# Twelve mask products, four k sums and six selection steps per pair of heads, regrouped into fewer, wider VectorE instructions

## The chip, the cores and the metric

One core of a Trainium2 chip runs the whole program. Its engines work side by side, each through its own list of instructions in order: PE (TensorE, matrix products and transposes; PEld is its weight load), DVE (VectorE, element-wise work and reductions), ACT (ScalarE, exponentials, casts and copies), POOL (GpSimd) and SP (SyncE), the last two used here for issuing DMA transfers. The metric is device time in microseconds (us); the kernel before took 453.29, 449.48 and 452.31 in three runs, median 452.31.

## The reference, cut to what matters

Block-sparse attention over batch 4, 8 heads, 768 positions, head size 64, and after it a Fourier mixing layer with a two-layer dense part.

```python
k_rep = k.reshape(B, H, 12, 64, D).mean(axis=3)          # one mean key per block of 64
gate = einsum('bhsd,bhnd->bhsn', q, k_rep)               # 768 x 12 per head
gate = where(pos // 64 >= n, gate, -1e9)
sel = three highest blocks of each row, and its own block
scores = q @ k.T / 8, kept where the block is selected and j <= i, else -1e9
attn = softmax(scores); out = attn @ v
x = out with the heads side by side                      # (4, 768, 512)
u = x + real(fft(fft(x, axis=1), axis=2))
un = layernorm(u)
result = u + relu(un @ w_ch1) @ w_ch2                    # 512 -> 2048 -> 512
```

## The kernel before, in words

Heads are taken two at a time (a pair, `hp`, of heads `e` = 0 and 1), so each of the four batches has four pairs. The 768 positions are six tiles of 128. For one pair:

- `stage_A` transposes q and k on TensorE (six tiles each, three to a PSUM tile), copies q transposed to `qt` (VectorE, fp32) and casts q and k to half precision (ScalarE). VectorE sums each block of 64 keys out of the same PSUM tile into `kr24`, 24 columns: head 0 in rows 0 to 63 and columns 0 to 11, head 1 in rows 64 to 127 and columns 12 to 23, the rest zero (L212, L231 to L235). Four reductions of 64 partitions do it.
- `stage_B` multiplies `qt` with `kr24` to gate scores of both heads, adds the causal term `cz24`, takes the eight largest of each row of 12 (twelve `max`, L251), and for each head turns "at least the third largest, or the own block" into 0 or -60000 in three steps (L252, L255, L256).
- `stage_C` transposes these rows on TensorE and copies them (L266) below the 64 rows of each head's q, so that one product of 76 rows gives scores with the selection in them. The k side holds 0/1 rows there.
- `stage_D_scores` computes the transposed scores, key tile `jt` by query columns, causal part only: 2688 columns a head, laid out by the list `BANKS` in five groups of 512 columns and one of 128, each in one PSUM bank (three buffers). ScalarE takes the exponential of a group in one instruction. Then VectorE multiplies each 128x128 diagonal tile with a triangular 0/1 mask (L293); the six diagonal tiles of a head lie in five of the six groups.
- `stage_D_av` multiplies with v (21 products of 65 columns a head, the last column gives the sums) and divides (L313, L314).

`gen_post` does the mixing of a batch: two products with cosine and sine (L350, L351), the second transform (L371, L372), residual and statistics, a short chain of 6-value instructions for the inverse deviation (L384 to L401), the normalisation (L408), transposes and copies (L415, L417), and the first dense product (L426, L427). `gen_post2` is the second dense product (L441, L443).

`drive` advances these as generators in turn: while batch b's attention runs, batch b-1 is in `gen_post` and batch b-2 in `gen_post2`. Batch 0's attention has only weight loads beside it. After the last attention, `gen_post(3)` runs beside `gen_post2(2)`, and `gen_post2(3)` ends the program. The framework's scheduler puts the instructions of each engine in order when the program is built, by program order and by when it expects operands to be ready, and adds the waits; a PSUM tile is read by ScalarE and VectorE one after the other.

Constants come by DMA. `emit_rest_consts` puts `cz24` and `own01` on the sync queue, behind pair 0's q and k and ahead of pair 2's q and k, which wait for a free buffer (two buffers each).

Of the kernel before, what the change touches and what calls it, by code (L numbers as in the profile page):

```python
# [11 lines left out]
FP = mybir.dt.float32  # L12
F16 = mybir.dt.float16
BF = mybir.dt.bfloat16

NEG = -60000.0
# [3 lines left out]
def _consts_np():  # L20
    S = 768
    DM = 512
    NB = 12
    KH = 386
    s = np.arange(S)
# [16 lines left out]
    own01 = ((s // 64)[:, None] == nn[None, :]).astype(np.float16)  # L42
    IndR = (nn[:, None] == (s[None, :] // 64)).astype(np.float16)
    return dict(CS=CS, SS=SS, CD=CD, SD=SD, ident32=ident32, ident16=ident16,
                ltri=ltri, ut01=ut01, cz24=cz24, own01=own01, IndR=IndR)
# [3 lines left out]
def kernel(  # L49
# [27 lines left out]
    spool = ctx.enter_context(tc.tile_pool(name="small", bufs=8))  # L77
# [12 lines left out]
    own01 = cpool.tile([128, NST, NB], F16, tag="c_own", name="own01")  # L90
# [21 lines left out]
    def emit_rest_consts():  # L112
        nc.sync.dma_start(cz24, dr["cz24"].ap().rearrange("(st p) n -> p st n", p=128))
        nc.sync.dma_start(own01, dr["own01"].ap().rearrange("(st p) n -> p st n", p=128))
# [41 lines left out]
    def emit_attn_dma(b, hp, qk_only=False, v_only=False):  # L156
# [25 lines left out]
        [(0, 0, 512)],  # L182
        [(0, 512, 768), (4, 512, 768)],
        [(1, 128, 640)],
        [(1, 640, 768), (3, 384, 768)],
        [(2, 256, 768)],
        [(5, 640, 768)],
    ]
    OFF = {}
    PT_W = 0  # L190
    for bank in BANKS:
        for (jt, a0, a1) in bank:
            if jt not in OFF:
                OFF[jt] = PT_W - (a0 - 128 * jt)
            PT_W += a1 - a0
    assert PT_W == 2688

    def gen_attention(b):
# [4 lines left out]
        def stage_A(hp):  # L203
# [8 lines left out]
            nc.vector.memset(kr24, 0.0)  # L212
            d["qt"], d["qg"], d["kI"], d["kr24"] = qt, qg, kI, kr24
            for who in range(2):
                src = qn if who == 0 else kn
                for g in range(2):
# [11 lines left out]
                    else:  # L228
                        nc.scalar.copy(out=kI[0][0:64, cols], in_=flat[0:64])
                        nc.scalar.copy(out=kI[1][0:64, cols], in_=flat[64:128])  # L230
                        for e in range(2):  # L231
                            nc.vector.tensor_reduce(
                                out=kr24[64 * e:64 * e + 64, 12 * e + 6 * g:12 * e + 6 * g + 6],
                                in_=ps[64 * e:64 * e + 64].rearrange("p a (x c) -> p a x c", x=2),
                                axis=mybir.AxisListType.X, op=mybir.AluOpType.add)  # L235

        def stage_B(hp):
# [20 lines left out]

        def stage_C(hp):
# [3 lines left out]
            for st in range(NST):  # L263
                nc.tensor.transpose(gt[0:44, st, :], gmp[:, st, :], id16)
# [4 lines left out]
        def stage_D_scores(hp):  # L269
# [5 lines left out]
            for bi, bank in enumerate(BANKS):  # L275
                wid_bank = sum(a1 - a0 for (_, a0, a1) in bank)
                for e in range(2):
# [3 lines left out]
                    diags = []  # L281
                    for (jt, a0, a1) in bank:
# [4 lines left out]
                        if a0 == 128 * jt:  # L287
                            diags.append(po + co)
# [3 lines left out]
                    for dof in diags:  # L292
                        nc.vector.tensor_tensor(out=pt[:, dof:dof + 128], in0=pt[:, dof:dof + 128],  # L293
                                                in1=ut01, op=mybir.AluOpType.mult)
                po += wid_bank

        def stage_D_av(hp):
            d = P[hp]
            v16 = d["v16"]
            for e in range(2):  # L300
# [4 lines left out]
                for jt in range(NST):  # L305
                    for st in range(jt, NST):
                        nc.tensor.matmul(av[:, st, 0:65],  # L307
                                         pt[:, OFF[jt] + 128 * (st - jt):OFF[jt] + 128 * (st - jt) + 128],
# [200 lines left out]
```

## Time and profile before

The profiled execution has a span of 449.5 us from its first to its last instruction; the lowest of the three runs is 449.48, the median 452.31. Mean granted TensorE clock of the core: 0.897 of full speed.

| engine | busy us | share of the span | instructions |
|---|---|---|---|
| PE | 402.2 | 89% | 2806 |
| PEld | 245.3 | 55% | 2806 |
| DVE | 308.3 | 69% | 1059 |
| ACT | 170.0 | 38% | 363 |
| POOL | 41.2 | 9% | 61 |

The chain of work that ended last is 80% PE, 7% DVE, 6% DMA and 5% ACT. Busy time is a sum over stages with different limits; an engine's idle time costs something only where the chain goes through it. PE's ends are modelled, since its instructions are pipelined. Batch 0's attention takes about the first 78 us, batch 1's ends near 159, batch 2's near 259, batch 3's near 358.

### The profile page before, as it was taken

The numbers are of one execution on the slowest core, as the hardware profiler recorded it, in microseconds if no ns is written. First come the engines' busy times: TensorE is split into PE (matmuls) and PEld (weight loads), VectorE is DVE, ScalarE is ACT, GpSimd is POOL, SyncE is SP. The second block draws the span as 40 slices with busy tenths as digits, with TensorE's granted clock in tenths as the row PEclk, the third lists the DMA queues.
The fourth block names the chain that finished last, engine by engine and source line by source line (L and its number), as shares of the span: only waits on it lengthen the run. The fifth ranks groups of instructions, "written<-read, shape, count | busy, mean of one in ns | idle before, by whom it ended". The sixth has DMA issues, their size and how long they took to land.

```text
span 449.5 us, 7427 instructions
## 1 busy us (share of the span) xinstructions
PE 402.2 (89%) x2806; PEld 245.3 (55%) x2806; DVE 308.3 (69%) x1059; ACT 170.0 (38%) x363; POOL 41.2 (9%) x61
## 2 busy tenths in 40 slices
PE   6518999898799999997899999996999999959996
PEld 2517756555466656454566656544665654436542
DVE  0446786799988855688898855688888733477711
ACT  1607678748533343137633244045644110010000
POOL 6705112000011110000001200000000000000000
PEclk9655558999599999999599999998699999969999
DMA  9999994833022262334022264010000011000011
GB/s 164 226 226 185 196 138 26 152 70 69 3 19 19 20 103 73 79 95 94 0 19 20 20 110 115 33 39 4 1 1 2 1 47 48 23 23 1 0 71 71
DMA packets 84980, 29.30 MB, mean 65 GB/s; under 512 B 78064, under 2 KB 80336, under 8 KB 84944
## 3 DMA queue, kind: packets, MB, share of 16 engines
q0 software_dynamic: 29184, 9.73, 18.3%
q1 hardware_dynamic: 52416, 18.28, 17.3%
q10 hardware_dynamic: 3344, 0.82, 1.1%
q8 instruction: 22, 0.36, 0.3%
q14 instruction: 14, 0.11, 0.1%
HBM read 29.87 MB, written 6.29 MB: 80 GB/s over the span
## 4 chain that ended last, share of the span: by engine, by line
PE 80%; DVE 7%; DMA 6%; ACT 5%; issue 1%; SPq 1%; ACTq 0%
DMA qn_2_181<-in_q_dram 3%; DMA id_74<-c_ident 1%; DMA qn_0_99<-in_q_dram 1%; PE ch_5_5338 L441 1%; PE ch_4_5319 L441 1%; PE ch_1_5262 L441 1%; PE ch_4_4879 L441 1%; PE ch_1_4758 L441 1%; PE ch_2_3565 L441 1%; PE ch_1_2230 L441 1%; PE ch_3_5300 L441 1%; PE ch_2_5281 L441 1%; PE ch_5_4918 L441 1%; PE ch_3_4840 L441 1%; PE ch_2_4799 L441 1%
## 5 line engine op out<-in xcount | busy, mean ns | idle before, releaser
L426 PEld LDWEIGHTS <-w_sb 128*128 128x128 f16 x256 | 25.1, 98 | 25.8 <-issue 0.6
L427 PEld LDWEIGHTS <-w_sb 128*128 128x128 f16 x256 | 25.0, 98 | 6.1 <-issue 0.7
L178 POOL DMA_DIRECT2D v_0_0_91<-in_v_dram x4 | 3.4, 854 | 121.0 <-PE av_0_0_2836 L307 65.3
L130 ACT COPY unT_0_4993<-unt_0_5003 128x768 f16<-128x768 f16 x1 | 0.8, 799 | 27.2 <-PE unt_0_5003 L415 27.2
L283 PEld LDWEIGHTS <-kI_1_88 76*128 76x128 f16 x32 | 4.1, 132 | 10.6 <-issue 10.1
L283 PEld LDWEIGHTS <-kI_1_84 76*128 76x128 f16 x32 | 4.1, 131 | 9.7 <-issue 9.2
L220 PE MATMUL tp_2_0_0_302<-id_74,qn_2_181 128*128 128x128 f32 x3 | 0.9, 430 | 9.5 <-DMA qn_2_181<-in_q_dram 9.5
L109 PE MATMUL warmps<-warm_src 128*128 128x512 f16 x22 | 6.9, 486 | 1.2 <-DVE v_0_2_93 L119 1.2
L178 POOL DMA_DIRECT2D v_0_1_92<-in_v_dram x4 | 3.3, 826 | 34.3 <-PE av_1_0_1773 L307 12.3
L283 PEld LDWEIGHTS <-kI_0_87 76*128 76x128 f16 x32 | 3.5, 111 | 4.6 <-issue 2.4
L220 PE MATMUL tp_0_0_0_194<-id_74,qn_0_99 128*128 128x128 f32 x3 | 0.9, 430 | 5.6 <-DMA id_74<-c_ident 5.6
L178 POOL DMA_DIRECT2D v_0_2_93<-in_v_dram x4 | 3.3, 828 | 27.8 <-PE av_2_0_1958 L307 10.8
L415 PE MATMUL unt_0_5003<-id_75,x_3400 128*128 128x128 f16 x6 | 1.7, 288 | 4.5 <-DVE x_3400 L408 4.5
L220 PEld LDWEIGHTS tp_2_0_0_302<-id_74,qn_2_181 128*128 128x128 f32 x3 | 0.5, 213 | 9.6 <-issue 9.6
L283 PEld LDWEIGHTS <-kI_0_83 76*128 76x128 f16 x32 | 3.6, 112 | 3.8 <-issue 1.3
L109 PEld LDWEIGHTS <-warm_src 128*128 128x128 f16 x22 | 2.6, 121 | 5.0 <-issue 2.5
L415 PEld LDWEIGHTS <-x_3400 128*128 128x128 f16 x24 | 2.1, 131 | 5.7 <-DVE x_3400 L408 5.3
L226 ACT CAST qg_0_0_190<-tp_0_0_0_194 64x384 f16<-64x384 f32 x1 | 0.5, 473 | 12.4 <-DVE qT_0_0_189 L225 12.4
L225 DVE COPY qT_0_2_297<-tp_2_0_0_302 128x384 f32<-128x384 f32 x1 | 0.6, 558 | 6.6 <-PE tp_2_0_0_302 L220 6.6
L283 PEld LDWEIGHTS <-kI_2_89 76*128 76x128 f16 x32 | 3.3, 107 | 3.0 <-issue 1.8
L225 DVE COPY qT_0_0_189<-tp_0_0_0_194 128x384 f32<-128x384 f32 x1 | 0.6, 557 | 6.2 <-PE tp_0_0_0_194 L220 6.2
L283 PEld LDWEIGHTS <-kI_2_85 76*128 76x128 f16 x32 | 3.3, 104 | 2.7 <-issue 0.6
(2748 smaller groups left out, 1418.4 us busy)
## 6 DMA issues: line engine op xcount, KB each, us to landing
w_sb<-in_moe_w_ch_dram POOLq DMA_DIRECT2D x8, 256.0 KB, 9.4
w_sb<-in_moe_w_ch_dram POOLq DMA_DIRECT2D x4, 512.0 KB, 16.7
out_dram<-u_943 SPq DMA_DIRECT2D x6, 256.0 KB, 2.4
out_dram<-u_2123 SPq DMA_DIRECT2D x6, 256.0 KB, 2.0
out_dram<-u_3417 SPq DMA_DIRECT2D x6, 256.0 KB, 2.0
out_dram<-u_4694 SPq DMA_DIRECT2D x6, 256.0 KB, 2.0
cs_sb<-c_CS POOLq DMA_DIRECT2D x1, 579.0 KB, 7.5
ss_sb<-c_SS POOLq DMA_DIRECT2D x1, 579.0 KB, 8.8
```

The source lines that it names most:

```text
L109: nc.tensor.matmul(wps, wsrc[:, 0:128], wsrc, start=True, stop=True)
L130: eng.copy(out=dst, in_=src)
L178: nc.gpsimd.dma_start(out=v16_t[e][sl][:, :, 0:64], in_=v[b, h].rearrange("(jt p) d -> p jt d", p=128))
L220: nc.tensor.transpose(ps[:, i, :], src[:, st, :, :].rearrange("p h d -> p (h d)"), id32)
L225: nc.vector.tensor_copy(out=qt[:, cols], in_=flat)
L226: nc.scalar.copy(out=qg[0][0:64, cols], in_=flat[0:64])
L283: nc.tensor.matmul(sp[:, co:co + (a1 - a0)], kI[e][0:76, 128 * jt:128 * (jt + 1)], qg[e][0:76, a0:a1], start=True, stop=True)
L415: nc.tensor.transpose(tps[:, st, :], un16[:, st, 128 * dt:128 * (dt + 1)], id16)
L426: nc.tensor.matmul(ha, w1s, unT[dt][:, 0:512], start=(dt == 0), stop=(dt == NDT - 1))
L427: nc.tensor.matmul(hb, w1s, unT[dt][:, 512:768], start=(dt == 0), stop=(dt == NDT - 1))
L441: nc.tensor.matmul(cps, hT[it][:, 128 * st:128 * (st + 1)], w2_sb[:, it, :], start=(it == 0), stop=(it == NIT - 1))
```

## The change

Three things in the attention part, with the constants that they need.

- The list `BANKS` is rearranged: the first four diagonal tiles of a head fill the first group, the last two stand at the head of the second, and what lies off the diagonal follows. The diagonal tiles of a group are multiplied in one instruction, the mask being repeated by its access pattern. A dictionary `COL` by key tile and query tile replaces `OFF`. Scores of a head are 13 matmuls in place of 8.
- The k sums are taken for both heads in one reduction of 128 partitions into `kr12`, and one product with a 0/1 constant `half24` spreads them over the 24 columns of `kr24`.
- The selection works on both heads at once: "less than the third largest" in place, then one instruction that multiplies by -60000 and by a constant `other24`, 0 in the own block and 1 elsewhere. The tile `gmp` is 64 columns a row tile in place of 44, and the pool of small tiles has 6 buffers in place of 8 (4 for `mx8`).

```diff
-    own01 = ((s // 64)[:, None] == nn[None, :]).astype(np.float16)
+    other = ((s // 64)[:, None] != nn[None, :]).astype(np.float32)
+    other24 = np.concatenate([other, other], axis=1)
+    half24 = ((jj[:, None] // 64) == (np.arange(2 * NB)[None, :] // NB)).astype(np.float32)
...
-    spool = ctx.enter_context(tc.tile_pool(name="small", bufs=8))
+    spool = ctx.enter_context(tc.tile_pool(name="small", bufs=6))
...
         nc.sync.dma_start(cz24, dr["cz24"].ap().rearrange("(st p) n -> p st n", p=128))
-        nc.sync.dma_start(own01, dr["own01"].ap().rearrange("(st p) n -> p st n", p=128))
+        nc.sync.dma_start(half24, dr["half24"].ap())
+        nc.sync.dma_start(other24, dr["other24"].ap().rearrange("(st p) n -> p st n", p=128))
...
     BANKS = [
-        [(0, 0, 512)],
-        [(0, 512, 768), (4, 512, 768)],
-        [(1, 128, 640)],
-        [(1, 640, 768), (3, 384, 768)],
-        [(2, 256, 768)],
-        [(5, 640, 768)],
+        [(0, 0, 128), (1, 128, 256), (2, 256, 384), (3, 384, 512)],
+        [(4, 512, 640), (5, 640, 768), (4, 640, 768), (0, 128, 256)],
+        [(0, 256, 768)],
+        [(1, 256, 768)],
+        [(2, 384, 768), (3, 512, 640)],
+        [(3, 640, 768)],
     ]
...
-            nc.vector.memset(kr24, 0.0)
+            kr12 = apool.tile([128, NB], FP, tag="kr12", name=f"kr12_{b}_{hp}")
...
-                        for e in range(2):
-                            nc.vector.tensor_reduce(
-                                out=kr24[64 * e:64 * e + 64, 12 * e + 6 * g:12 * e + 6 * g + 6],
-                                in_=ps[64 * e:64 * e + 64].rearrange("p a (x c) -> p a x c", x=2),
-                                axis=mybir.AxisListType.X, op=mybir.AluOpType.add)
+                        nc.vector.tensor_reduce(
+                            out=kr12[:, 6 * g:6 * g + 6],
+                            in_=ps.rearrange("p a (x c) -> p a x c", x=2),
+                            axis=mybir.AxisListType.X, op=mybir.AluOpType.add)
+            nc.vector.tensor_tensor(out=kr24.rearrange("p (e n) -> p e n", e=2),
+                                    in0=kr12.rearrange("p (o n) -> p o n", o=1)
+                                    .to_broadcast([128, 2, NB]),
+                                    in1=half24.rearrange("p (e n) -> p e n", e=2),
+                                    op=mybir.AluOpType.mult)
...
-            gmp = apool.tile([128, NST, 44], F16, tag="gmp", name=f"gmp_{b}_{hp}", bufs=4)
+            gmp = apool.tile([128, NST, 64], F16, tag="gmp", name=f"gmp_{b}_{hp}", bufs=4)
             d["gmp"] = gmp
-            for e in range(2):
-                gm = gmp[:, :, 32 * e:32 * e + NB]
-                mx8 = spool.tile([128, NST, 8], FP, tag="mx8", name=f"mx8_{b}_{hp}_{e}")
-                for st in range(NST):
-                    nc.vector.max(out=mx8[:, st, :], in_=gsb[:, st, NB * e:NB * (e + 1)])
-                nc.vector.tensor_tensor(out=gm, in0=gsb[:, :, NB * e:NB * (e + 1)],
-                                        in1=mx8[:, :, 2:3].to_broadcast([128, NST, NB]),
-                                        op=mybir.AluOpType.is_ge)
-                nc.vector.tensor_tensor(out=gm, in0=gm, in1=own01, op=mybir.AluOpType.max)
-                nc.vector.tensor_scalar(out=gm, in0=gm, scalar1=1.0, scalar2=-NEG,
-                                        op0=mybir.AluOpType.subtract, op1=mybir.AluOpType.mult)
+            mx8 = spool.tile([128, NST, 2, 8], FP, tag="mx8", name=f"mx8_{b}_{hp}", bufs=4)
+            for st in range(NST):
+                for e in range(2):
+                    nc.vector.max(out=mx8[:, st, e, :], in_=gsb[:, st, NB * e:NB * (e + 1)])
+            g4 = gsb.rearrange("p s (e n) -> p s e n", e=2)
+            nc.vector.tensor_tensor(out=g4, in0=g4,
+                                    in1=mx8[:, :, :, 2:3].to_broadcast([128, NST, 2, NB]),
+                                    op=mybir.AluOpType.is_lt)
+            nc.vector.scalar_tensor_tensor(
+                out=gmp.rearrange("p s (e n) -> p s e n", e=2)[:, :, :, 0:NB], in0=g4, scalar=NEG,
+                in1=other24.rearrange("p s (e n) -> p s e n", e=2),
+                op0=mybir.AluOpType.mult, op1=mybir.AluOpType.mult)
...
-                    for dof in diags:
-                        nc.vector.tensor_tensor(out=pt[:, dof:dof + 128], in0=pt[:, dof:dof + 128],
-                                                in1=ut01, op=mybir.AluOpType.mult)
+                    if ndiag:
+                        dg = pt[:, po:po + 128 * ndiag].rearrange("p (n c) -> p n c", c=128)
+                        nc.vector.tensor_tensor(
+                            out=dg, in0=dg,
+                            in1=ut01.rearrange("p (o c) -> p o c", o=1)
+                            .to_broadcast([128, ndiag, 128]),
+                            op=mybir.AluOpType.mult)
```

## Rows read from the trace of the kernel before

**Rows 1.** Busy time by stage: batch 0, 1 and 3; us busy (count) per engine, clock, DMA.

```profile
0.00:78.00 78.00, 58.20 (x394) 41.12 (x395) 41.26 (x198) 41.80 (x85) 28.00 (x45) 0.65 1.07 166
...
78.00:159.00 81.00, 73.73 (x592) 47.33 (x591) 70.24 (x254) 40.52 (x88) 6.65 (x9) 0.94 0.35 50
...
259.00:358.00 99.00, 93.38 (x696) 57.22 (x695) 76.42 (x258) 41.35 (x90) 0.00 (x0) 0.95 0.14 34
```

**Rows 2.** Waits of PE: who waited for whom, us in total, times, longest.

```profile
PE tp_2_0_0_302 L220 <- DMA qn_2_181<-in_q_dram: 9.5, 1, 9.5
...
PE ya_3_1126 L350 <- DVE kr_1_1_1064 L232: 0.4, 1, 0.4
```

**Rows 3.** Busy time in half-microsecond slices, columns as in rows 1.

```profile
114.00:114.50 0.50, 0.00 (x0) 0.00 (x0) 0.49 (x6) 0.00 (x0) 0.00 (x0) 0.93 0.00 0
...
312.00:312.50 0.50, 0.00 (x0) 0.00 (x0) 0.50 (x1) 0.00 (x0) 0.00 (x0) 0.90 0.00 0
...
322.50:323.00 0.50, 0.50 (x18) 0.50 (x16) 0.47 (x2) 0.50 (x2) 0.00 (x0) 0.86 0.00 0
```

**Rows 4.** Timeline of batches 1 and 3: start, us, engine, instruction [idle before, releaser].

```profile
114.98 0.59 PE L283 MATMUL sc_1_1_0_1462<-qg_1_1_1063,kI_1_88 76*128 76x512 f16 x1 [2.89 <-DVE qg_1_1_1063 L266]
...
311.32 0.48 ACT L230 CAST kI_3_90<-tp_3_1_1_3951 64x384 f16<-64x384 f32 x1
...
311.98 1.12 DVE L232 TENSOR_REDUCE kr_3_3_3927<-tp_3_1_1_3951 64x6 f32<-64x384 f32 x2
...
313.68 0.55 DVE L266 COPY qg_1_0_3593<-gt_1_3989 12x768 f16<-12x768 f16 x1
...
314.28 0.59 PE L283 MATMUL sc_1_0_0_4046<-qg_1_0_3593,kI_1_84 76*128 76x512 f16 x1 [4.18 <-DVE qg_1_0_3593 L266]
...
317.47 2.83 DVE L408 TENSOR_SCALAR x_2106<-u_3417,stat_2_3998,rstd_2_3999 128x512 f16<-128x512 f32 x6
```

**Rows 5.** A line's instructions (min/median/max ns), then timeline of batch 3, by size.

```profile
L397 DVE TENSOR_TENSOR t_2_4025<-yi_4020 x2: 166/166/166, 315.8 to 316.6; 128x6 f32<-128x6 f32 x2
...
307.13 0.69 DVE L373 TENSOR_TENSOR u_3417<-mx_5_3914,x_2106 128x512 f32<-128x512 f32 x1
...
308.20 0.55 DVE L225 COPY qT_3_3_3924<-tp_3_0_1_3936 128x384 f32<-128x384 f32 x1
...
309.69 0.31 DVE L244 TENSOR_TENSOR gsb_2_3966<-g_2_3959,cz_77 128x144 f32<-128x144 f32 x1 [0.34 <-PE g_2_3959 L241]
```

**Rows 6.** Timeline of batch 3: the selection of pair 2.

```profile
310.03 0.54 DVE L251 MAX8 mx_3_2_0_3969<-gsb_2_3966 128x8 f32<-128x12 f32 x6
...
313.40 0.16 DVE L256 TENSOR_SCALAR gmp_2_3968<-gmp_2_3968 128x72 f16<-128x72 f16 x1
...
314.26 0.23 DVE L252 TENSOR_TENSOR gmp_2_3968<-gsb_2_3966,mx_3_2_1_3979 128x72 f16<-128x72 f32 x1
```

**Rows 7.** Timeline of batch 3: mask products, pair 0.

```profile
306.64 0.22 DVE L293 TENSOR_TENSOR ptl_0_0_3850<-ptl_0_0_3850,ut_76 128x128 f16<-128x128 f16 x1
...
306.78 0.22 DVE L293 TENSOR_TENSOR ptl_0_1_3851<-ptl_0_1_3851,ut_76 128x128 f16<-128x128 f16 x1
```

**Rows 8.** PE: timeline, chain of waits (batch 2), weight loads of the page.

```profile
303.40 0.38 PE L283 MATMUL sc_0_0_3_3878<-qg_0_0_3468,kI_0_83 76*128 76x128 f16 x2
...
303.62 0.38 PE L372 MATMUL mx_4_3904<-sd_sb,zR_2_3560 128*128 128x512 f16 x1
...
228.43 0.44 PE gt_2_2956 L264 x6
...
237.01 0.64 PE av_1_0_3067 L307 x21
...
L426 PEld LDWEIGHTS <-w_sb 128*128 128x128 f16 x256 | 25.1, 98 | 25.8 <-issue 0.6
```

**Rows 9.** Timeline: issues on the sync queue, start and us.

```profile
12.66 0.37 SPq L114 DMA_DIRECT2D own_78<-c_own  x1
...
15.23 0.37 SPq L167 DMA_DIRECT2D qn_2_181<-in_q_dram  x1
```

More of the change, by code (lines that the diff above doesn't have):

```diff
@@ L41, in _consts_np @@
     cz24 = np.concatenate([cz, cz], axis=1)
-    own01 = ((s // 64)[:, None] == nn[None, :]).astype(np.float16)
+    other = ((s // 64)[:, None] != nn[None, :]).astype(np.float32)
+    other24 = np.concatenate([other, other], axis=1)
+    half24 = ((jj[:, None] // 64) == (np.arange(2 * NB)[None, :] // NB)).astype(np.float32)
     IndR = (nn[:, None] == (s[None, :] // 64)).astype(np.float16)
     return dict(CS=CS, SS=SS, CD=CD, SD=SD, ident32=ident32, ident16=ident16,
-                ltri=ltri, ut01=ut01, cz24=cz24, own01=own01, IndR=IndR)
+                ltri=ltri, ut01=ut01, cz24=cz24, other24=other24, half24=half24, IndR=IndR)
 @with_exitstack
@@ L89 @@
     cz24 = cpool.tile([128, NST, 2 * NB], FP, tag="c_cz24", name="cz24")
-    own01 = cpool.tile([128, NST, NB], F16, tag="c_own", name="own01")
+    other24 = cpool.tile([128, NST, 2 * NB], FP, tag="c_other", name="other24")
+    half24 = cpool.tile([128, 2 * NB], FP, tag="c_half", name="half24")
     eps1 = cpool.tile([128, 1], FP, tag="c_eps1", name="eps1")
@@ L181 @@
     BANKS = [
-        [(0, 0, 512)],
-        [(0, 512, 768), (4, 512, 768)],
-        [(1, 128, 640)],
-        [(1, 640, 768), (3, 384, 768)],
-        [(2, 256, 768)],
-        [(5, 640, 768)],
+        [(0, 0, 128), (1, 128, 256), (2, 256, 384), (3, 384, 512)],
[4 more added lines that the diff above has]
+        [(3, 640, 768)],
     ]
-    OFF = {}
+    COL = {}
     PT_W = 0
@@ L192 @@
         for (jt, a0, a1) in bank:
-            if jt not in OFF:
-                OFF[jt] = PT_W - (a0 - 128 * jt)
+            for i in range(a0, a1, 128):
+                COL[jt, i // 128] = PT_W + i - a0
             PT_W += a1 - a0
-    assert PT_W == 2688
+    assert PT_W == 2688 and len(COL) == 21
     def gen_attention(b):
@@ L263, in stage_C @@
             for st in range(NST):
-                nc.tensor.transpose(gt[0:44, st, :], gmp[:, st, :], id16)
+                nc.tensor.transpose(gt[0:44, st, :], gmp[:, st, 0:44], id16)
             for e in range(2):
@@ L280, in stage_D_scores @@
                     co = 0
-                    diags = []
+                    ndiag = 0
                     for (jt, a0, a1) in bank:
@@ L287, in stage_D_scores @@
                         if a0 == 128 * jt:
-                            diags.append(po + co)
+                            ndiag += 1
                         co += a1 - a0
@@ L307, in stage_D_av @@
                         nc.tensor.matmul(av[:, st, 0:65],
-                                         pt[:, OFF[jt] + 128 * (st - jt):OFF[jt] + 128 * (st - jt) + 128],
+                                         pt[:, COL[jt, st]:COL[jt, st] + 128],
                                          v16[e][:, jt, 0:65],
```

## The prediction

> **What bounds the kernel now.** I read the busy time by stage first. Over batch 3's attention, beside which the transform of batch 2 and the second dense product of batch 1 run, TensorE is busy 93.4 of 99 us and VectorE 76.4 [rows 1]. So TensorE is the bound, and what VectorE saves is worth something only where TensorE waits for it. Batch 1 is closer to a tie: 73.7 and 70.2 of 81 us. Batch 0 runs alone, TensorE at a mean granted clock of 0.65, that is for much of it at the lower level (1.2 GHz).
>
> The list of waits says where that is: the longest, 9.5 us in batch 0, is for a q load; 0.4 us in batch 1 is for k sums [rows 2]. The long ones that this change can touch lie in one place of each later batch: scores of pair 1 wait 2.9 us in batch 1 and 4.2 in batch 3 (batch 2 has its twin), each for the copy of the transposed selection rows on VectorE [rows 4].
>
> Then the clock in half-microsecond slices [rows 3]. In batch 3 it falls at about 312.4, 2.3 us after TensorE ran dry (its wait of 4.2 us ended at 314.28, so began at 310.1), and is back at about 322.6: ten microseconds at 1.2 GHz. In batch 1 it falls at about 114.4, 2.3 us into the wait of 2.9. An idle stretch therefore costs twice, itself and slower work behind it.
>
> Last the order on VectorE in that place [rows 4]: two pairs of k sums (1.12 us each; the second stands), the second not before ScalarE's last cast out of the same bank (ended 311.80); then the rest of pair 2's selection; only then the copy at 313.68, which TensorE awaits. Behind the copies come the layer-norm chain and the six normalisations from 317.47 to 320.30, on which the next dense product hangs. From 310 to 320 VectorE is the bound, though TensorE is for the batch.
>
> **The change, part by part**, per pair of heads, 16 pairs in all.
>
> *k sums.* Four reductions of 64 partitions become two of 128. A 64x384 reduction takes 0.56 us (1.12 a pair [rows 4]); a 128x384 copy of the same 384 columns 0.55 [rows 5], so partitions cost nothing, and a reduction stays 0.56. Added is a product of 24 values, between 0.17 (6 values) and 0.31 (144 values) [rows 5]: I take 0.19, near the small one. 4 x 0.56 - 2 x 0.56 - 0.19 = 0.93 us saved; the memset that goes is left out. The product waits for both reductions, and the gate products wait for it; they come a round later, so this is hidden.
>
> *Selection.* Per head three 72-value operations of 0.16 to 0.23 us, some 1.2 us per pair [rows 6]. Instead two of 144 values: nearest is the 144-value addition, 0.31, so 0.62; saved 0.55. Bounds of the two-step operation, which no row shows: 0.17 to 0.62. The twelve maxima stay (six in 0.54).
>
> *Masks.* Twelve 128x128 products become two of 512 and two of 256 columns. One takes 0.22 alone and starts 0.14 after the one ahead when they queue [rows 7]. The repeated mask is in no row, so I bound it. With the 6-value product's 0.17 as the fixed part, 0.22 at 128 makes 0.44 ns a column in half precision; fp32 ones, from 0.31 at 144 to 0.69 at 512, take 1.03 ns [rows 5]. By the first slope 512 columns take 0.39 and 256 take 0.28; by the second, up to 0.69 and 0.43. I take the first, same operation and type: 2 x (0.39 + 0.28) = 1.34 against 12 x 0.22 = 2.64, saved 1.3 when apart (0.4 at the other bound); against 12 x 0.14 = 1.68 when queued, saved 0.3, or 0.6 lost.
> The Trainium skill's page "VectorE: DVE Perf Modes", section "What auto-detection actually checks", lets a two-source product run at two elements a cycle if every operand is 16-bit with step 1; the mask's inner step stays 1, so by it the lower figures hold. No run here has shown it for a repeated operand.
>
> Together about 2.8 us of VectorE busy time per pair, 45 us in all (bound 30).
>
> *Scores.* Per head 13 matmuls in place of 8, hence 160 more in all, each with a weight load; columns and exponentials stay the same. A bank of two pieces (128 + 384) starts at 303.40 and the next matmul at 303.62: 0.22 us, the time of one 512-column matmul, and 21 weight loads with 65 columns each follow every 0.030 us [rows 8]. So I take nothing. Upper bound: six 128-column transposes with weights of their own take 0.44 us, 0.073 each, against 0.0545 for a quarter of 0.22. Eight such pieces a head, 32 heads over the batches: 256 x 0.0185 = 4.7 us.
> The Trainium skill's page "TensorE: Matmul & The Clock Gate", section "Back-to-back issue gap", speaks against the change: a stream of weight load and 128-column matmul runs at about 81 ns each. By that, as an estimate, 256 x (81 - 54.5) ns = 6.8 us would be added; the scores here lie between other matmuls, and the 30 ns pairs show weight loads overlapped.
>
> *Constants.* The sync queue gets one load more ahead of pair 2's q load, and a selection constant of four times the bytes in as many rows. Issues there stand 2.6 us apart [rows 9], with 768 rows each; the new one has 128, a sixth, so 0.4 us, bounds 0 and 2.6. Pair 2's q is what TensorE awaits for 9.5 us, so this counts in full. Against it I set what batch 0's four pairs save on VectorE, no row putting it on the path: net nothing. If the small constant came late, VectorE would stop at the first product with everything queued behind; its turn comes only after pair 0's transposes, copies and k sums. Fewer buffers for small tiles cost nothing: the reciprocals have two a pair.
>
> **On the path.** Batches 2 and 3: the second reduction can start at 311.84 and ends at 312.40 instead of 313.10; the maxima fill the gap ahead of it, and the copy starts at about 312.55, 1.1 us earlier. Fusing takes another 0.4 off what precedes the layer-norm; against that, four wide masks (0.31 each when queued, 1.24) now fall into that chain, where six small ones (0.84) stood: 0.4 lost. Net -1.1 us each. TensorE's idle stretch is then 3.1 us, still beyond the 2.3 at which the clock fell.
> Batch 1: the same 1.1; 0.5 in the one other stretch where TensorE waits for a reduction [rows 2], which gets half as long; 0.4 from masks queued between 100 and 110 us: -2.0. Its idle stretch shrinks by more than the 0.6 us that lie between 2.9 and 2.3, so I expect the clock to hold. Worth, by batch 3's times, between 1.2 us (half of the 2.3 from the normalisation's end at 320.30 to 322.6) and 4.2 (half of the 8.3 from 314.28): I take 1.5, near the low end, since VectorE sets the pace until the normalisation ends.
> Sum: -1.1 - 1.1 - 2.0 - 1.5 = -5.7. The profiled execution has a span of 449.5, and a run of 449.48 is in the list, so nothing visible lies around it; it becomes 443.8. The median of the runs shown is 452.31, 2.8 higher; on that footing 446.6, and I say **446.5**.
>
> **Rivals.**
> *The clock holds in all three places.* If the order puts a copy into the gap between the two reductions, as batch 1's order did, the idle stretch falls to about 2 us. Then 1.5 to 4.2 us more in each of batches 2 and 3: 443.5 to 438. For it: the freed gap of 0.4 us. Against: the copy takes 0.55 and attention's selection has gone ahead of it so far. Chance 0.22.
> *Nothing to see.* The wide masks run at the fp32 slope (queued 0.14 + 384 x 1.03 ns = 0.54 us instead of 0.31 by the other slope; four in the layer-norm chain make 0.9 us a batch, 2.7 in three), and the clock falls as before: 452.3 - (5.7 - 2.7 - 1.5) = 450.8. This is also the case in which the change does not relieve what it says. Chance 0.18.
> *Slower: the quartered scores wait for their weights.* If each added weight load cost its own 0.098 us (its duration beside the dense product [rows 8]), 160 x 0.098 = 15.7 us are added: 452.3 - 5.7 + 15.7 = 462. It decides from (5.7 + 4.5) / 160 = 0.064 us a piece, above which the kernel is over 1% slower. The 30 ns pairs speak against it. Chance 0.06.
> *The rest*: the scheduler's order on the engines is made anew from the changed lengths, and can bring a wait that the old trace does not have: 448 to 458, chance 0.08.
>
> **Numbers.** The forecast has 0.46, spread over 443 to 450: 0.30 of it below 447.8, which is 1% under 452.3, about what a measurement can tell from no change. Faster: 0.30 + 0.22 + 0.01 = 0.53. Same: 0.16 + 0.18 + 0.03 = 0.37. Slower: 0.06 + 0.04 = 0.10. The range 439 to 454 leaves out the weight-load case, the worst of the rest and the best of the clock case, some 0.15.
>
> **What would show it.** Right: 512-column masks at 0.39, reductions on 128 partitions at 0.56, VectorE some 45 us less busy, pair 1's first wait near 3.1 us in batches 2 and 3 and under 2.3 in batch 1, no fall of the clock at 114. Wrong: masks near 0.7; quarter matmuls more than 0.07 us apart; clock falls at the three places unchanged; a wait of VectorE for a constant in batch 0.

## The result: faster, by more than forecast

The changed kernel takes 438.43 us (median of 4, 436.71 to 441.94) against 451.14 for the kernel before beside it (449.48 to 453.29): a ratio of 0.974 [0.968, 0.980]. The forecast was 446.5, so the sign was right, and the time lies 0.6 us under the low end of the range. (The forecast stood on 452.31 for the kernel before; 0.974 of that is 440.5, inside the range.) A second set of runs (e8, below) gave 0.9805 [0.974, 0.987]. The ratios leave out slow executions, those over 1.5% above the fastest of their kernel; medians and ranges hold all.

The profiled execution, the fastest of the four, has a span of 434.9 us (before 449.5) and a mean granted clock of 0.925 (before 0.897). Marks that every trace has, the first cast of a batch and the first store of a result, cut it into stages:

| us | before | after | |
|---|---|---|---|
| batch 0, to batch 1's first cast | 78.33 | 69.21 | -9.1 |
| batch 1, from there to the first store | 85.92 | 81.94 | -4.0 |
| batch 2, first store to first store | 99.42 | 98.66 | -0.8 |
| batch 3 | 98.98 | 98.36 | -0.6 |
| last stage, to the last batch's first store | 66.51 | 66.45 | -0.1 |

Busy time by stage, after, columns as in [rows 1]:

```profile
0.00:78.00 78.00, 58.21 (x488) 43.81 (x489) 38.21 (x156) 48.29 (x103) 28.14 (x45) 0.80 1.19 183
78.00:159.00 81.00, 76.91 (x648) 49.31 (x647) 62.48 (x194) 37.97 (x84) 6.54 (x8) 0.96 0.34 52
259.00:358.00 99.00, 94.85 (x734) 58.93 (x733) 66.63 (x200) 37.48 (x82) 0.00 (x0) 0.95 0.08 25
```

VectorE has 10 us less to do in batch 3's stretch, and TensorE is no less busy (94.9 us for 93.4): that stage hardly moved. The one clock that moved much is batch 0's, from 0.65 [rows 1] to 0.80 over the same 78 us.

Waits of TensorE, after (total, times, longest):

```profile
PE tp_2_0_0_297 L224 <- DMA qn_2_183<-in_q_dram: 6.9, 1, 6.9
...
PE sc_1_1_1_512 L292 <- ACT ptl_1_0_489 L299: 2.1, 1, 2.1
PE sc_1_0_0_3983 L292 <- DVE qg_1_0_3546 L275: 2.1, 1, 2.1
```

The wait for the q load is 2.6 us shorter than in [rows 2]. The dip of batch 3, the stretch in which TensorE runs dry ahead of pair 1's scores, is down from 4.2 us [rows 4] to 2.1 (and 0.9, below). The clock, in half-microsecond slices (it is the figure behind the five engines, 0.61 in the first row):

```profile
38.00:38.50 0.50, 0.50 (x8) 0.50 (x7) 0.50 (x2) 0.24 (x1) 0.00 (x0) 0.61 1.13 204
48.50:49.00 0.50, 0.50 (x6) 0.50 (x4) 0.50 (x2) 0.50 (x2) 0.00 (x0) 0.63 1.21 194
55.00:55.50 0.50, 0.50 (x12) 0.50 (x11) 0.35 (x2) 0.50 (x3) 0.00 (x0) 0.54 1.23 198
103.00:103.50 0.50, 0.50 (x9) 0.40 (x7) 0.50 (x5) 0.38 (x1) 0.00 (x0) 0.74 0.00 0
110.00:110.50 0.50, 0.50 (x13) 0.47 (x11) 0.19 (x1) 0.25 (x1) 0.00 (x0) 0.93 0.00 0
297.50:298.00 0.50, 0.00 (x0) 0.00 (x0) 0.47 (x4) 0.43 (x1) 0.00 (x0) 0.80 0.00 0
308.00:308.50 0.50, 0.37 (x11) 0.27 (x9) 0.50 (x2) 0.50 (x2) 0.00 (x0) 0.96 0.00 0
```

A slice that holds a change tells its moment: 0.61 is 0.11 us at the upper level and the rest at half. In batch 0 the clock comes back to the upper level at 38.4 us, falls at 48.6 and is back for good at 55.5; before, it came back at 70.1. In the dips it still falls (103.2, 297.8) and is back 7 and 10 us later; [rows 3] had ten.

The dip of batch 3, after, in order of time (start, us, engine, line, operation [idle before]):

```profile
294.25 0.47 ACT L233 CAST kI_3_87<-tp_3_1_0_3886 64x384 f16<-64x384 f32 x1 [1.54 <-PE tp_3_1_0_3886 L224]
...
296.98 0.56 DVE L235 TENSOR_REDUCE kr_3_3_3871<-tp_3_1_0_3886 128x6 f32<-128x384 f32 x1
...
297.72 0.55 DVE L275 COPY qg_1_0_3546<-gt_1_3926 12x768 f16<-12x768 f16 x1
298.30 0.56 DVE L235 TENSOR_REDUCE kr_3_3_3871<-tp_3_1_1_3893 128x6 f32<-128x384 f32 x1
298.78 0.30 DVE L260 TENSOR_TENSOR gsb_2_3908<-gsb_2_3908,mx_3_2_3911 128x144 f32<-128x144 f32 x1
298.99 0.18 DVE L239 TENSOR_TENSOR kr_3_3_3870<-kr_3_3_3871,half_79 128x24 f32<-128x24 f32 x1
299.18 0.55 DVE L275 COPY qg_1_1_3547<-gt_1_3926 12x768 f16<-12x768 f16 x1
299.76 0.31 DVE L263 SCALAR_TENSOR_TENSOR gmp_2_3910<-gsb_2_3908,other_78 128x144 f16<-128x144 f32 x1
...
300.06 0.42 DVE L303 TENSOR_TENSOR ptl_1_0_3981<-ptl_1_0_3981,ut_76 128x512 f16<-128x512 f16 x1
...
301.10 0.42 DVE L303 TENSOR_TENSOR ptl_1_1_3982<-ptl_1_1_3982,ut_76 128x512 f16<-128x512 f16 x1
...
301.59 0.29 DVE L303 TENSOR_TENSOR ptl_1_0_3981<-ptl_1_0_3981,ut_76 128x256 f16<-128x256 f16 x1
...
302.08 0.29 DVE L303 TENSOR_TENSOR ptl_1_1_3982<-ptl_1_1_3982,ut_76 128x256 f16<-128x256 f16 x1
...
303.09 2.83 DVE L421 TENSOR_SCALAR x_2076<-u_3371,stat_2_3935,rstd_2_3936 128x512 f16<-128x512 f32 x6
```

TensorE in the same stretch, its timeline:

```profile
298.32 0.58 PE L292 MATMUL sc_1_0_0_3983<-qg_1_0_3546,kI_1_85 76*128 76x128 f16 x4 [2.08 <-DVE qg_1_0_3546 L275]
299.79 0.59 PE L292 MATMUL sc_1_1_0_3990<-qg_1_1_3547,kI_1_89 76*128 76x128 f16 x4 [0.88 <-DVE qg_1_1_3547 L275]
...
308.97 0.38 PE L439 MATMUL ha_0_4135<-unT_0_3971,w_sb 128*128 128x512 f16 x1
```

The same marks before, as far as [rows 4] does not have them:

```profile
308.11 0.47 ACT L229 CAST kI_3_86<-tp_3_1_0_3943 64x384 f16<-64x384 f32 x1 [1.54 <-PE tp_3_1_0_3943 L220]
...
314.52 0.55 DVE L266 COPY qg_1_1_3594<-gt_1_3989 12x768 f16<-12x768 f16 x1
...
316.12 0.22 DVE L293 TENSOR_TENSOR ptl_1_0_4044<-ptl_1_0_4044,ut_76 128x128 f16<-128x128 f16 x1
...
316.73 0.22 DVE L293 TENSOR_TENSOR ptl_1_1_4045<-ptl_1_1_4045,ut_76 128x128 f16<-128x128 f16 x1
...
317.14 0.22 DVE L293 TENSOR_TENSOR ptl_1_0_4044<-ptl_1_0_4044,ut_76 128x128 f16<-128x128 f16 x1
...
323.73 0.38 PE L426 MATMUL ha_0_4196<-unT_0_4034,w_sb 128*128 128x512 f16 x1
```

Set against [rows 4]: the first copy now stands between the two reductions, and four wide mask products, in place of three small ones, stand ahead of the normalisation of the rows (L421). Counted from pair 3's first cast (294.25; before 308.11), the first copy comes at 3.47 us in place of 5.57, the second at 4.93 in place of 6.41, the normalisation at 8.84 in place of 9.36, and the dense layer's first matmul at 14.72 in place of 15.62. Two microseconds at the top of the queue are half of one at its end.

The scores, after, in the timeline: banks of four pieces start 0.22 to 0.23 us apart, as the bank of two did in [rows 8].

```profile
286.88 0.39 PE L292 MATMUL sc_0_0_0_3793<-qg_0_0_3422,kI_0_84 76*128 76x128 f16 x4
287.11 0.39 PE L292 MATMUL sc_0_1_0_3800<-qg_0_1_3423,kI_0_88 76*128 76x128 f16 x4
287.33 0.39 PE L292 MATMUL sc_0_0_1_3807<-qg_0_0_3422,kI_0_84 76*128 76x128 f16 x4
```

Their weight loads, from the page's groups (busy us, mean ns | idle before), 97 ns each ([rows 8] had 98):

```profile
L292 PEld LDWEIGHTS <-kI_2_90 76*128 76x128 f16 x52 | 4.2, 97 | 2.1 <-issue 1.3
```

The issues on the sync queue, after, with the small constant in front; [rows 9] had the q load at 15.23:

```profile
13.33 0.32 SPq L117 DMA_DIRECT2D half_79<-c_half  x1
...
15.45 0.38 SPq L171 DMA_DIRECT2D qn_2_183<-in_q_dram  x1
```

### The profile page after: what moved, and what is told of

It reads as the page before. It is cut to its first block, busy times and chain, and to the rows that moved or that the text cites. A ratio compares the mean times of both kernels' runs of the same rounds, so it can differ in the third digit from the quotient of the medians.

```text
span 434.9 us, 7521 instructions
## 1 busy us (share of the span) xinstructions
PE 393.6 (91%) x2966; PEld 246.4 (57%) x2966; DVE 276.3 (64%) x835; ACT 167.9 (39%) x363; POOL 41.2 (9%) x61
## 4 chain that ended last, share of the span: by engine, by line
PE 77%; ACT 6%; issue 6%; DMA 6%; DVE 4%; SPq 0%; ACTq 0%
DMA qn_2_183<-in_q_dram 3%; DMA qn_1_140<-in_q_dram 2%; PE ch_5_5276 L454 1%; PE ch_3_4778 L454 1%; PE ch_4_5257 L454 1%; PE ch_0_5181 L454 1%; PE ch_3_3626 L454 1%; PE ch_2_2240 L454 1%; PE ch_3_5238 L454 1%; PE ch_2_5219 L454 1%; PE ch_1_5200 L454 1%; PE ch_5_4856 L454 1%; PE ch_2_4737 L454 1%; PE ch_1_4696 L454 1%; PE ch_0_4655 L454 1%
## 5 line engine op out<-in xcount | busy, mean ns | idle before, releaser
L292 PEld LDWEIGHTS <-kI_1_85 76*128 76x128 f16 x52 | 5.2, 119 | 10.1 <-issue 9.8
L292 PEld LDWEIGHTS <-kI_1_89 76*128 76x128 f16 x52 | 5.5, 127 | 7.2 <-issue 7.1
L292 PEld LDWEIGHTS <-kI_0_88 76*128 76x128 f16 x52 | 4.4, 101 | 3.1 <-issue 1.3
L292 PEld LDWEIGHTS <-kI_0_84 76*128 76x128 f16 x52 | 4.5, 104 | 2.2
L292 PEld LDWEIGHTS <-kI_2_90 76*128 76x128 f16 x52 | 4.2, 97 | 2.1 <-issue 1.3
L292 PEld LDWEIGHTS <-kI_3_91 76*128 76x128 f16 x52 | 4.2, 97 | 2.0 <-issue 1.3
L292 PEld LDWEIGHTS <-kI_3_87 76*128 76x128 f16 x52 | 4.2, 97 | 1.4 <-issue 0.2
L292 PEld LDWEIGHTS <-kI_2_86 76*128 76x128 f16 x52 | 4.1, 97 | 1.3
```

Of the source, the lines that this page charges most:

```text
L292: nc.tensor.matmul(sp[:, co:co + (a1 - a0)], kI[e][0:76, 128 * jt:128 * (jt + 1)], qg[e][0:76, a0:a1], start=True, stop=True)
```

## Experiments

My first theory (A): batch 0 gained because the new order brings the clock back earlier, and the dips by the k sums. Rival (B): each part gives what it takes off VectorE. The first four kernels are the kernel before with one part each.

**e1, the selection alone** (is_lt and one two-step product over both heads, `other24` in place of `own01`).

> The kernel before with the one-pass selection alone (and the smaller pool of small tiles). Theory A, from the two traces: most of the gain, 9 of 14.6 us between the two profiled executions, lies in batch 0, where the engines' order came out anew and TensorE reached its upper clock at 38 us instead of 70; the dips of batches 1 to 3 gave 4.0, 0.8 and 0.6. By A the selection shortens the later dips by 0.4 us each at most, 1 us in all, and batch 0 gains some 6 us only if its trace shows the clock up before 50 us; without that 449 to 451, with it 443 to 446. Rival B, the time follows VectorE's saved work: of 32 us less busy the selection has about 9, so a quarter of the 12.7 us gain, 448, spread over all batches.

Measured: 0.998 [0.995, 1.002]. Nothing.

**e2, the new banks and the fused masks alone.**

> The kernel before with the rearranged groups and the wide mask products alone. Theory A: the dips of batches 1 to 3 come from k sums, selection and copies, not from masks; the waits of 4.2 us in batches 2 and 3 stay within 0.4, these batches change by under 0.5 us each, and what is gained lies in batch 0 by its new order (443 to 447 if the clock is up before 50 us there, 450 to 452 if not). Rival B, work: the masks have about 40% of the work saved, so 446, 1.5 us of it in each of batches 2 and 3.

Measured: 0.992 [0.989, 0.996].

**e3, the k sums alone** (two reductions of 128 partitions and the product with `half24`).

> The kernel before with the k sums of both heads in one reduction alone. Theory A: this is the edit that shortens the dips: the wait of pair 1's first scores falls from 4.2 to about 3.1 us in batches 2 and 3, batch 1 gets 2 to 4 us shorter, batches 2 and 3 0.5 to 1 each; with batch 0 unchanged 446 to 448. Rival B, work: about 15 of 32 us saved, so 445, evenly over the batches. Rival C, the added load ahead of pair 2's q delays batch 0: its first transposes of pair 2 start later than 31.7 us.

Measured: 0.990 [0.983, 0.996].

**e4, the new banks alone**, each 128x128 mask still on its own:

```
-        [(0, 0, 512)], [(0, 512, 768), (4, 512, 768)], ...
+        [(0, 0, 128), (1, 128, 256), (2, 256, 384), (3, 384, 512)], ...
```

> The kernel before with the rearranged groups, so 160 more score matmuls and weight loads, but the mask products one tile at a time. My prediction: the added matmuls cost nothing, at most 4.7 us (batches 2 and 3 unchanged within 0.5 us, or 1.2 us longer each at the bound). Rival, each added weight load costs its own 0.098 us: 15.7 us longer, 3.9 in each batch. Batch 0 may move either way by several us, by order and clock.

Measured: 0.996 [0.992, 0.999]. The 160 additional matmuls and weight loads cost nothing that can be seen.

The stages of these profiles, and of those further down, as in the first table. "Low" is twice (1 - granted clock) times the length of the stretch from 30 us to the end of batch 0, the time at the lower level; it is worked out from that stretch's row, of which three stand below the table. (In e6's 17 some 2 us come from an upper level of 0.95, see the end.)

| run | batch 0 | low | batch 1 | batch 2 | batch 3 | last |
|---|---|---|---|---|---|---|
| before | 78.3 | 40 | 85.9 | 99.4 | 99.0 | 66.5 |
| e1 selection | 78.7 | 45 | 85.0 | 98.9 | 98.6 | 67.9 |
| e3 k sums | 76.5 | 40 | 82.1 | 98.6 | 98.3 | 66.8 |
| e4 banks | 72.4 | 22 | 85.1 | 99.3 | 98.8 | 68.0 |
| e2 banks, masks | 70.5 | 14 | 85.4 | 99.7 | 99.0 | 67.7 |
| after | 69.2 | 15 | 81.9 | 98.7 | 98.4 | 66.5 |
| e8, after again | 72.6 | 28 | 81.7 | 98.4 | 98.4 | 68.0 |
| e5 | 78.6 | 40 | 85.8 | 99.4 | 99.0 | 66.5 |
| e9 | 81.4 | 44 | 85.6 | 99.3 | 99.0 | 66.4 |
| e6 | 69.1 | 17 | 83.1 | 99.5 | 97.6 | 66.0 |
| e7 | 68.5 | 17 | 81.4 | 98.3 | 97.7 | 65.9 |
| e10 | 71.2 | 27 | 81.3 | 98.2 | 98.2 | 66.9 |
| e11 | 70.0 | 20 | 81.6 | 98.4 | 97.2 | 67.1 |
| e12 | 74.0 | 34 | 80.8 | 96.4 | 96.1 | 65.9 |

The stretch behind 30 us in the kernel before, in e4 and in e8, columns as in [rows 1]:

```profile
30.00:78.33 48.33, 44.94 (x338) 32.66 (x339) 32.55 (x149) 32.64 (x67) 12.89 (x19) 0.59 0.94 137
```

```profile
30.00:72.42 42.42, 39.34 (x378) 31.44 (x379) 30.03 (x149) 31.54 (x67) 12.92 (x19) 0.74 1.11 159
```

```profile
30.00:72.57 42.57, 39.79 (x372) 31.33 (x370) 24.27 (x96) 32.66 (x67) 13.82 (x20) 0.67 1.09 159
```

Read down two columns. Batch 0 takes 68.5 to 74.0 us in every profile with the new banks and 76.5 to 81.4 in every one with the old. VectorE's work does not decide it: e3 and e2 keep VectorE busy for the same time in batch 0 (37.3 and 37.2 us, before 41.6), and one is long, the other short. The k sums alone give batch 1 its 4 us and batches 2 and 3 their 0.7 to 0.8; the banks give the last two nothing and batch 1 0.5 to 0.8, no more than the selection (0.9). B falls for batch 0. Over the 14 profiles batch 0 follows the low-clock time at 0.36 us per microsecond (correlation 0.95); TensorE is busy for nine tenths of that stretch. Part of this is built in, since a batch 0 that takes longer at the lower level also counts more low time. The kernel after alone, in its two profiles, has 15 and 28 us of it, 69.2 and 72.6 us of batch 0 (0.26 us per microsecond), the same batches 1 to 3 within 0.3 us, and a last stage of 66.5 and 68.0 us.

The executions that were not profiled settle more. The record has each one's mean clock over the whole run, and with it the low time, twice (1 - clock) times the span. Over 69 executions of the kernel before (one of 2149 us left aside) the time follows it at 0.27 us per microsecond (correlation 0.94), from 444.6 us at a clock of 0.919 to 453.5 at 0.890. A straight line through each kernel's executions, read where their low times meet (the executions scatter about their line by 0.4 to 1.4 us):

| low time of the whole run | before | e4 banks | e2 banks, masks | after | e1 selection | e3 k sums |
|---|---|---|---|---|---|---|
| 75 us | 446.1 | 445.5 | 445.9 | 439.5 | | |
| 85 us | 448.8 | | | | 447.6 | 443.4 |
| mean of the executions, us | 88 (69) | 75 (10) | 77 (10) | 76 (10) | 88 (10) | 86 (4) |

At equal clock the banks, with or without fused masks, are worth at most 0.6 us, the k sums 5.4 and the whole change 6.6. What the banks bring is the clock: 11 to 13 us less low time, some 3 us by that slope. The kernel before does nearly as well in those of its executions that have the clock without the change: five at 0.919 to 0.923 took 444.6 to 445.2 us, e4's three there 443.8 to 444.3. That this low time lies in batch 0 is read from the profiles: from 80 us on, it is 31 to 38 us in all seven of them up to e8.

**e5, e9: can the kernel before be given that clock?** Matmuls of zeros, overwritten by the real ones, fill waits of TensorE; e9 adds those in front of two score banks to those of e5:

```
+                    if b == 0 and hp == 2 and who == 0 and g == 0:
+                        for _ in range(18):
+                            nc.tensor.matmul(ps..., wsrc[:, 0:128], wsrc[:, 0:384], ...)
+                    if b == 0 and e == 0 and (hp, bi) in ((0, 1), (2, 0)):   # e9
+                        for _ in range(6 if bi else 2):
+                            nc.tensor.matmul(sp, wsrc[:, 0:128], wsrc[:, 0:wid_bank], ...)
```

> The kernel before with one addition and no part of the change: 18 matmuls of zeros, 128x384, whose results are overwritten, stand on TensorE ahead of pair 2's first transposes in batch 0, where TensorE otherwise sits idle for the q load (9.5 us, rows 2). They take about 18 x 0.32 = 5.8 us at the low clock, so they end before the load lands. Theory A (the change's gain in batch 0 is TensorE's clock coming back at 38 us in place of 70 us): here too the clock comes back before 45 us, the first cast of batch 1 moves from 78.3 us to 70 to 73 us, and the time falls by 5 to 8 us, to a ratio of 0.982 to 0.989. Rival B (the gain is VectorE's saved work or the order of the banks itself): the clock may come back earlier, but the cast stays within 1 us of 78 us and the ratio is 0.998 to 1.002. Rival C (the load's landing sets batch 0): the same as B unless the load itself moves.

Measured: 1.002 [0.998, 1.005]; the clock was up from 25.7 to 29.1 us and for 3.4 us at 53, and back only at 73.5. The lever did not move, so this tells nothing between the theories.

> The kernel before, no part of the change, with the 18 fills of run e5 in batch 0's load wait and 8 more zero matmuls, overwritten like those: six of 128x256 ahead of the third score bank (in the kernel before, TensorE then waits 1.04 us at 42.99 us for the first exponential) and two of 128x512 ahead of pair 2's first bank (a wait of 0.36 us at 61.69 us). Over the nine profiled executions so far, batch 0 (to the first cast of batch 1) ends at 68.5 to 72.6 us where the low clock takes 14 to 29 us of the stretch behind 30 us, and at 76.5 to 78.7 us where it takes 40 to 45 us, whatever the kernel: about 0.35 us per microsecond of low clock. Theory A (batch 0's gain is that clock): if the clock comes back before 60 us here, the cast comes at 70 to 75 us and the ratio is 0.982 to 0.993; if it does not come back before 70 us, the cast stays at 78 us and the ratio at 0.998 to 1.004, which tells nothing between the theories. Rival B (the banks' order itself sets batch 0): the cast stays at 78 us with the clock back early.

Measured: 0.989 [0.985, 0.992], no part of the change in it. Nine of ten executions took 442.7 to 446.7 us at a mean clock of 0.927 to 0.938 over the run (before, beside it: 0.890 to 0.916, mostly 0.90). The one that was profiled is the tenth: 455.09 us at 0.896, clock back at 76 us, cast at 81.4. That the nine had their higher clock in batch 0 is therefore inferred, from its being the one stage with that much low time, not seen. They took about 3 us more than the line of the kernel before, drawn on to their clock, would give; whether the fills cost that was not tested.

**e6, e7, e8: holding the clock in the dips.** In the kernel after, 9 and 4 such matmuls ahead of pair 1's first score banks of batches 1 to 3 (e6); the same with 18 in the load wait and 20 in the last stage's wait (e7); the kernel after itself (e8).

> The kernel after with 13 matmuls of zeros, 128x512, in each of batches 1 to 3, ahead of pair 1's first score matmuls of either head (9 and 4); they write the score banks and are overwritten. They stand where TensorE waits for the two copies of the selection (2.1 and 0.9 us), 13 x 0.22 = 2.8 us. Theory A (in batches 2 and 3 the shorter wait is given back because the clock still falls and the 8.5 us of work behind it runs at half rate): with the wait filled the clock stays at 1.0 and each of the three batches gets 2.5 to 4.5 us shorter, 8 to 13 us in all, a ratio of 0.945 to 0.957 to the kernel before. Rival B (behind the wait ScalarE's exponentials set the pace, twelve of 0.69 us for a pair): the clock stays up and the batches keep their length, ratio 0.972 to 0.977. Rival C: three fills ahead of the selection's transposes and the late ones delay the chain, 0.3 to 0.9 us a batch, ratio 0.976 to 0.982; this is possible beside A.

> The fills of the run before it, with the same 18 fills in batch 0's load wait, and 20 matmuls of zeros of 128x512 in the last stage where TensorE waits 4.5 us for the normalised rows (clock low from 383.5 to 390 us). Theory A: batch 0 holds the clock from the load on; as the kernel after already has it for most of the stretch behind 38 us, that is worth 2 to 4 us; the tail's low 6.5 us become full-rate, worth 1 to 3 us; ratio 0.935 to 0.95. Rival B (the clock is not what sets either stage): the same ratio as the run before it, within 0.003.

> The kernel after as it is, beside the two above on the same chip. All theories: a ratio of 0.968 to 0.98; it is the base for the two runs above it.

Measured: 0.974 [0.969, 0.979], 0.976 [0.970, 0.982] and 0.9805 [0.974, 0.987]. In e6's batch 3 the clock stays at 1.00:

```profile
290.00:300.00 10.00, 9.92 (x73) 6.23 (x71) 7.16 (x25) 8.38 (x19) 0.00 (x0) 1.00 0.08 28
300.00:310.00 10.00, 8.33 (x98) 5.29 (x97) 9.46 (x35) 7.17 (x16) 0.00 (x0) 1.00 0.00 1
```

and the stage is 0.8 us shorter, not 2.5 to 4.5 (the dense layer's first matmul comes 13.21 us behind the cast, 1.5 earlier). TensorE now idles 1.7 us of the second ten: it gets through the scores sooner and then waits for the rows that VectorE (busy for 9.46 us) normalises at the same distance from the cast, 8.75 us. Theory A for the dips falls: half-rate work hides a VectorE queue of nearly the same length. In e7 the last stage ran at the upper level throughout and took 65.9 us, 0.6 less than after, where 1 to 3 had been expected.

**e10, e11: shortening that queue.** e10 makes pair 1's masks wait, by a data dependence, until the normalised rows are transposed; e11 leaves out one Newton step of the inverse root.

```
+            nc.vector.scalar_tensor_tensor(out=held01, in0=unT[NDT - 1][:, 0:128], scalar=0.0,
+                                           in1=ut01, op0=mult, op1=add)   # e10: mask for pair 1, b > 0
-        for _it in range(2):
+        for _it in range(1):   # e11
```

> The kernel after with one order changed: in batches 1 to 3 pair 1's four mask products wait (they read a copy of the mask that is made from the last copy of the normalised rows) until VectorE has normalised the batch before; the added copy is one operation of 0.2 us. Theory C (the dip of batches 1 to 3 ends with VectorE's queue: sums, selection, mask products, the 13 small operations and the six products of 2.83 us of the normalisation; the change took about 1.7 us of sums and selection out of it and put 4 mask products, 2 x 0.42 + 2 x 0.29 = 1.42 us, into it): each of the three stages gets 0.9 to 1.4 us shorter than in the kernel after (81.8, 98.5 and 98.4 us between first stores in its two profiles), 3 to 4 us in all, a ratio to the kernel before of 0.965 to 0.972. Rival D (half-rate work behind the dip sets its end): stages within 0.3 us of the kernel after, ratio 0.973 to 0.981. Rival E: the products held back delay pair 1's products with v and the stages get longer by up to 1 us.

> The kernel after with one of the two Newton steps of the inverse root left out (a part of the computation is left out here): four operations of 0.17 us, 0.2 us from start to start, fewer in VectorE's normalisation of each batch. Theory C (VectorE's queue ends the dip): 0.7 to 0.9 us less in each of the stages of batches 1 to 3 and in the tail, where TensorE waits for the same rows: 2.8 to 3.6 us in all. Rival D (half-rate work, or the exponentials, end the dip): 0.8 us less in the tail alone, the three stages within 0.2 us of the kernel after.

Measured: 0.971 [0.967, 0.976] and 0.972 [0.968, 0.976]. In both the normalisation of batch 3 starts 0.8 to 0.9 us earlier behind the cast (7.96 and 8.03), so the masks did stand in that queue with 0.9 us. But the dense layer follows only where the clock is back: in e10 (low until 309.6) its first matmul comes at 14.59, 0.1 us earlier, and in e11's batch 3 (low until 305.8; after, until 308.0) at 13.50, 1.2 us earlier. C is half right, and D too.

**e12: both at once**, e10's order and e7's fills.

> The kernel after with pair 1's mask products held back as in run e10 and with the fills of run e7 (load wait, the three dips, the last stage). In e10 and e11 the normalisation of batches 1 to 3 came 0.8 us earlier behind pair 3's first cast (first product at 7.96 and 8.03 us in place of 8.83) but the first matmul of the network came only 0.1 to 0.5 us earlier where the clock was low, and 1.2 us earlier where it had come back; in e6 with the clock up and the normalisation as in the kernel after it came 1.4 us earlier. Theory F (two things end the dip, VectorE's normalisation and half-rate work, and each hides the other): with both taken away the first matmul of the network comes 12.2 to 12.8 us behind the cast (14.7 in the kernel after), stages 2 and 3 take 96 to 97.5 us between first stores, and the time is 431 to 435 us, a ratio of 0.957 to 0.967. Rival G (behind the dip something else sets the stage, so that the two don't add): stages of 97.5 to 98.3 us, ratio 0.969 to 0.976, as runs e6, e7 and e10.

Measured: 435.37 us, 0.960 [0.953, 0.968] (the medians of all executions give 0.965). The three marks in batch 3, the cast, the normalisation and the dense layer:

```profile
295.59 0.47 ACT L239 CAST kI<-tp 64x384 f16<-64x384 f32 x1 [1.54 <-PE tp L230]
...
303.57 2.83 DVE L439 TENSOR_SCALAR x<-u,stat,rstd 128x512 f16<-128x512 f32 x6
...
308.02 0.38 PE L466 MATMUL ha<-unT,w_sb 128*128 128x512 f16 x1
```

7.98 and 12.43 us behind the cast; stages 2 and 3 take 96.4 and 96.1 us, 2.3 less than after. The two shortenings together give more than the sum of each alone (e7 0.4 and 0.7 us in these stages, e10 0.5 and 0.2): VectorE's queue and the half-rate matmuls each hid the other. F came, G fell. This kernel beats the one before, and its interval lies below both of the kernel after, if barely below the first. Its profiled execution had a long batch 0 (low for 34 us); its fastest took 429.79.

## Why the prediction was right, and where it was wrong

**Single costs: right.** A reduction of 128 partitions takes 0.56 us, the product 0.18, the two-step selection 0.31 (taken: 0.56, 0.19, 0.31). The wide masks take 0.42 and 0.29 (taken 0.39 and 0.28), 0.51 ns a column, near the half-precision slope of the prediction and half of the fp32 one. So the Trainium skill's page "VectorE: DVE Perf Modes", section "What auto-detection actually checks", holds for a repeated mask here. VectorE is 32 us less busy, not 45. The k sums alone take off 17.1 (forecast 15), the banks and masks 12.0 (21), the selection 3.3 (9). Line by line the last two gave more, 16.4 and 8.8 us; but the small products and steps had overlapped with what stood beside them (0.22 us long, 0.14 apart [rows 7]), and the engine's busy time counts that once. The mask case lies between "queued" and "apart".

**Scores at nothing: right.** Four pieces take 0.22 to 0.23 us, 56 ns each, and e4 is not slower. The 81 ns of the Trainium skill's page "TensorE: Matmul & The Clock Gate", section "Back-to-back issue gap", are not seen in these banks of four.

**Batch 0, "net nothing": wrong, and the step that failed.** I weighed a load against VectorE's work and did not ask what the new order does to the clock, though [rows 1] showed 0.65 there. Batch 0 fell by 9.1 us, 5.8 in the second profile. The load itself landed 2.7 us earlier although its issue was 0.2 later, but e1 had its first exponential 2.1 us earlier too and gained nothing, so that alone is not the cause. The new banks alone give 5.9 of it with the clock back at 52 us, and masks fused 7.8. How the banks bring the clock back is not settled: the old order had a wait of 1.04 us at 42.99 that the new lacks, and e9, which fills it, points there; but the new has a wait of its own (2.1 us until 47.73, the clock fell 0.9 us behind its end), and one kernel's return varies by 13 us between two executions.

**Batch 1, -3.5: size right, reason half wrong.** It gave 4.0. The clock did not hold; it fell, for 7 us instead of 10. In e3 it fell for 10 us and the stage still lost 3.8. From cast to cast TensorE idled 81.3 - 74.0 = 7.3 us before and 77.3 - 72.6 = 4.7 after: the waits gave 2.6, where I had 2.0. The other 1.4 us TensorE was busy for less; in e3, with the clock low for 10 us, it was 1.3, so the shorter low stretch does not explain them.

**Batches 2 and 3, -1.1 each: 0.8 and 0.6.** The top of the dip did better than forecast: the copies came 2.1 and 1.5 us earlier, because one slipped between the reductions. The term "four wide masks fall into that chain, 0.4 lost" was too small: from the second copy to the normalisation it is now 3.91 us against 2.95, 0.96 more, and e10 takes 0.88 of it away again. Two readings in it were wrong and partly cancelled. Before, three small masks stood there, not six (0.41 us from start to start, not 0.84); and two of the four wide ones have 256 columns, so that they take 1.10 and not 1.24. And TensorE's half-rate work kept some of the rest (e10 against e12).

**The rivals.** What "the clock holds in all three places" built on came true, a copy between the two reductions and an idle stretch of about 2 us (2.1), and the clock fell all the same. In batches 2 and 3 it fell 1.3 and 1.6 us after TensorE ran dry (in batch 3 at 296.24), in batch 1 some 4 us after, with scores in between; I had made a limit of the 2.3 us of two rows. That 438.4 lies in that rival's range is therefore chance. Weight loads and the fp32 slope did not come. The rest, an order made anew, did, on the good side.

**Sum.** Without batch 0 I forecast 5.7, and 5.5 came between the two profiled executions; the remaining 9 us are batch 0's. These two lie far apart in clock (0.897 and 0.925). At equal clock, over all executions, the change is worth 6.6 us, near the 5.7; the clock gave the rest, some 3 us on average. One reading beside the sum was wrong and harmless: where the record has both, a time is 1.8 us above its span (436.71 and 434.9), so the span of 449.5 was not the run of 449.48; the 5.7 were taken off the median.

## What to carry over

Where one stage runs at the lower clock with its engine nearly always busy, ask first what a new order does to the clock there, and compare kernels at equal clock: between the two profiled executions batch 0 was 9.1 of 14.6 us, over all executions the clock was about a third of the gain (3 of the 9.8 us between the means), and it varies between executions of one kernel. Where two things of nearly equal length end a stretch, taking one away shows nothing; take away both before calling either harmless. Work that is fused comes all at once and early: ask what it now stands in front of.

## What the runs showed that was not expected

The same kernel on the same data returned to the upper clock in batch 0 at 55.5 us in one execution and 68.3 in another, with 3.4 us between their batches 0. In one execution of e6 the upper stretches had a granted clock of 0.95, between the levels, from 55 to 274 us; batches 1 and 2 were 0.8 to 1.4 us longer than in the kernel after:

```profile
120.00:130.00 10.00, 9.93 (x100) 6.16 (x99) 7.89 (x20) 4.86 (x12) 1.64 (x2) 0.95 0.32 22
```
